# Convolution on VectorE, tokens scattered to regions per expert, and expert blocks started sequence by sequence

## The chip, the cores and the metric

The kernel runs on one core of one Trainium2 chip. The metric is the device time of the program in microseconds (us), median of the runs shown. One further execution was profiled; every duration below comes from it. Engines are named as in the profile: PE (TensorE; PEld its weight loads), DVE (VectorE), ACT (ScalarE), POOL (GpSimd) and SP (SyncE, which here only issues DMAs).

## What is computed

Eight sequences of 3584 tokens with 192 channels are convolved along time with 7 taps (a softmax of the weights, one set per head of 24 channels). Each convolved token is then sent to one of 8 experts, a two-layer network 192 to 1024 to 192 with ReLU, and scaled by its gate probability. A token takes the expert of its own best logit, unless its local gate is at least 0.5: then it takes the expert of the token before it.

```python
x_unf = x_pad[:, idx, :].reshape(B, S, K, H, group)          # causal window of 7
x = np.einsum('hk,bskhg->bshg', w, x_unf).reshape(B, S, D)
logits = np.einsum('bsd,de->bse', x, w_gate)
local_gate = 1.0 / (1.0 + np.exp(-np.einsum('bsd,de->bse', x, w_local).squeeze(-1)))
for b in range(B):
    prev_e = -1
    for s in range(S):
        fresh_e = int(np.argmax(logits[b, s]))
        e = fresh_e if s == 0 or local_gate[b, s] < 0.5 else prev_e
        prev_e = e
        h = np.maximum(x[b, s] @ w1[e], 0.0)
        out[b, s] = softmax(logits[b, s])[e] * (h @ w2[e])
```

## The kernel before

Three stages run one after the other; a scheduler sets the order of the instructions within each.

**Convolve and route** (`convolve_and_route`), over the sequences. `conv_bands` first builds banded 128 x 128 matrices on DVE and POOL (L73, L78, L80). A sequence lies in SBUF with tokens over partitions, 28 tiles of 128; PE multiplies it with the bands (L167, L169), ACT and DVE copy the result from PSUM into `y_sb` (L172, L174), PE transposes it (L180), ACT and DVE copy that (L184, L186), and PE forms the 9 logits (L189). `route` turns the logits into a one-hot of the expert per token with some 30 small DVE instructions and four tiny PE transposes; the carry of the expert from token to token is a running maximum over a key. The sequence goes to DRAM as `rows`.

**Place** (`place`), once, after all eight sequences: a running sum over all tokens gives each its slot, experts start at multiples of 256 slots, and 224 rounds of three DVE compares and one PE matmul (L355 to L361) turn "slot of token" into "token of slot", `slot_tok`. A block of 256 slots has one expert; there are 119 blocks.

**Experts** (`experts`), over the 119 blocks. Per block: SP loads the expert's weights `w1b` and `w2b` (L387, L389), POOL gathers 2 x 128 rows by `slot_tok` with indirect DMAs (L394); PE does the first layer (`hidden`: L415 on 128 channels, L424 on the other 64 in two 64-row tiles), the transposes of the next block (`turn`, L404), then the second layer (`output`, L439). ACT and DVE share the ReLU copies `hT` (L432, L430: two each) and the gated copies `o_sb` (L447, L445); DVE also copies the transposes, `xT` (L407). POOL scatters `o_sb` to the output with two indirect DMAs (L450). Weights are loaded two blocks ahead, with three buffers.

Of the kernel before, what the change touches and what calls it, by code (L numbers as in the profile page):

```python
# [9 lines left out]
BF16 = mybir.dt.bfloat16  # L10
# [39 lines left out]
def conv_bands(nc, cst, scr, weight):  # L50


    w = scr.tile([P, H, KC], F32, name="w")
    nc.sync.dma_start(out=w, in_=weight.partition_broadcast(P))
# [8 lines left out]
    c = scr.tile([P, H, KC], F32, name="c")  # L63
    nc.vector.tensor_tensor(c, w, bcast(ws, KC), op=Alu.mult)

    band = cst.tile([P, H, P], F32, name="band")
    pband = cst.tile([P, H, P], F32, name="pband")
    for dst, j0, shift in ((band, 0, 0), (pband, 1, P)):
        for j in range(j0, KC):

            m = scr.tile([P, P], F32, name="m", bufs=2)
            nc.gpsimd.memset(m, 0.0)
            nc.gpsimd.affine_select(out=m, in_=m, compare_op=Alu.not_equal, fill=1.0,  # L73
                                    base=shift - j, pattern=[[1, P]], channel_multiplier=-1)
            for h in range(H):
                tap = c[:, h, KC - 1 - j:KC - j]
                if j == j0:
                    nc.vector.tensor_scalar(dst[:, h, :], m, tap, None, Alu.mult)  # L78
                else:
                    nc.vector.scalar_tensor_tensor(dst[:, h, :], m, tap, dst[:, h, :],  # L80
                                                   Alu.mult, Alu.add)
    return band, pband
# [3 lines left out]
def kernel(  # L86
# [5 lines left out]
    w1: bass.AP,  # L92
    w2: bass.AP,
# [3 lines left out]
    keep = ctx.enter_context(tc.tile_pool(name="keep", bufs=1))  # L97
    dram = ctx.enter_context(tc.tile_pool(name="dram", bufs=1, space=DRAM))

    rows = dram.tile([N + 1, DG], F32, name="rows")  # L100

    ident = keep.tile([P, P], F32, name="ident")
    make_identity(nc, ident)

    oh_all = keep.tile([P, E, T], F32, name="oh_all")
    slot_tok = keep.tile([P, NS], I32, name="slot_tok")
    blk_e = keep.tile([1, NB], I32, name="blk_e")

    with ExitStack() as one:
        convolve_and_route(one, tc, x, weight, wgl, rows, ident, oh_all)  # L110
    with ExitStack() as two:
        place(two, tc, oh_all, slot_tok, blk_e)
    with ExitStack() as three:
        experts(three, tc, w1, w2, out, rows, ident, slot_tok, blk_e)


def convolve_and_route(ctx, tc, x, weight, wgl, rows, ident, oh_all):
    nc = tc.nc
    cst = ctx.enter_context(tc.tile_pool(name="cst", bufs=1))
    xs = ctx.enter_context(tc.tile_pool(name="xs", bufs=2))  # L120
    ys = ctx.enter_context(tc.tile_pool(name="ys", bufs=2))
    sm = ctx.enter_context(tc.tile_pool(name="sm", bufs=2))
    cps_p = ctx.enter_context(tc.tile_pool(name="cps_p", bufs=2, space=PSUM))
    tps_p = ctx.enter_context(tc.tile_pool(name="tps_p", bufs=2, space=PSUM))
    lps_p = ctx.enter_context(tc.tile_pool(name="lps_p", bufs=2, space=PSUM))
    rps_p = ctx.enter_context(tc.tile_pool(name="rps_p", bufs=1, space=PSUM))

    def load_x(b):
        x_sb = xs.tile([P, NT + 1, D], F32, name="x_sb")
        nc.gpsimd.memset(x_sb[:, 0, :], 0.0)  # L130
        for s in range(0, NT, CB):
            nc.sync.dma_start(out=x_sb[:, 1 + s:1 + s + CB, :],
                              in_=x[b, s * P:(s + CB) * P].rearrange("(j p) d -> p j d", p=P))
        return x_sb

    x_next = load_x(0)
    wg = cst.tile([DH, 2, E + 1], F32, name="wg")
    nc.scalar.dma_start(out=wg.rearrange("p k e -> p (k e)"), in_=wgl)
    zrow = cst.tile([1, DG], F32, name="zrow")
    nc.vector.memset(zrow, 0.0)  # L140
    nc.scalar.dma_start(out=rows[N:N + 1, :], in_=zrow)
    with tc.tile_pool(name="scr", bufs=1) as scr:
        band, pband = conv_bands(nc, cst, scr, weight)


    si = cst.tile([P, NT], I32, name="si")
    nc.gpsimd.iota(si, pattern=[[P, NT]], base=0, channel_multiplier=1)
    sf = cst.tile([P, NT], F32, name="sf")
    nc.vector.tensor_copy(sf, si)
    nc.vector.tensor_scalar(sf, sf, float(E), float(E + 1), Alu.mult, Alu.add)  # L150

    ii = cst.tile([P, E], I32, name="ii")
    nc.gpsimd.iota(ii, pattern=[[1, E]], base=0, channel_multiplier=0)
    ef = cst.tile([P, E], F32, name="ef")
    nc.vector.tensor_copy(ef, ii)
    ed = cst.tile([P, E], F32, name="ed")
    nc.vector.tensor_scalar(ed, ef, -1.0, float(E), Alu.mult, Alu.add)

    def conv(x_sb):
        y_sb = ys.tile([P, NT, DG], F32, name="y_sb")  # L160
        lps = lps_p.tile([P, NT, E + 1], F32, name="lps")
        for s in range(0, NT, CB):
            for h in range(H):
                hc = slice(h * GS, (h + 1) * GS)
                yc = slice(1 + h * GS, 1 + (h + 1) * GS)
                cps = cps_p.tile([P, CB, GS], F32, name="cps")
# [4 lines left out]
                if h % 2:  # L171
                    nc.vector.tensor_copy(y_sb[:, s:s + CB, yc], cps)  # L172
                else:
                    nc.scalar.copy(y_sb[:, s:s + CB, yc], cps)  # L174
            nc.gpsimd.tensor_copy(y_sb[:, s:s + CB, 1 + D:], y_sb[:, s:s + CB, 1 + P:1 + D])
        for j in range(0, NT, 2):
            tps = tps_p.tile([DH, 2, 2, P], F32, name="tps")
            for u in range(2):
                for k in range(2):
                    nc.tensor.transpose(tps[:, u, k, :], y_sb[:, j + u, 1 + k * DH:1 + (k + 1) * DH],  # L180
                                        identity=ident)
            yT = sm.tile([DH, 2, 2, P], F32, name="yT", bufs=3)
            if (j // 2) % 2:
                nc.vector.tensor_copy(yT, tps)  # L184
            else:
                nc.scalar.copy(yT, tps)  # L186
            for u in range(2):
                for k in range(2):
                    nc.tensor.matmul(lps[:, j + u, :], lhsT=yT[:, u, k, :], rhs=wg[:, k, :],  # L189
                                     start=(k == 0), stop=(k == 1))  # L190
        return y_sb, lps

    def route(b, y_sb, lps):
        lt = sm.tile([P, NT, E + 1], F32, name="lt")
# [25 lines left out]
        nc.vector.reciprocal(rs, rs)  # L220

        rps = rps_p.tile([P, 512], F32, name="rps")
        nc.tensor.transpose(rps[:NT, :P], key, identity=ident)
        row = sm.tile([NT, P], F32, name="row")
        nc.vector.tensor_copy(row, rps[:NT, :P])
        last = sm.tile([NT, 1], F32, name="last")
        nc.vector.tensor_reduce(last, row, axis=AX.X, op=Alu.max)
        nc.tensor.transpose(rps[:1, P:P + NT], last, identity=ident[:NT, :NT])  # L230
# [30 lines left out]
    for b in range(B):  # L261
# [4 lines left out]
        if held:  # L266
            route(b - 1, *held)
# [232 lines left out]
```

## Time and profile before

| | us |
|---|---|
| three runs, median (lowest to highest) | 1920.5 (1916.2 to 1920.5) |
| the profiled execution | 1925.5 |
| its span, first to last instruction | 1923.8 |
| PE busy | 1795.3 (93%) |
| DVE busy | 595.0 (31%) |
| ACT busy | 257.8 (13%) |
| POOL busy | 510.1 (27%) |
| bytes moved by DMA | 293.8 MB, 153 GB/s over the span |

The page cuts the span into 40 slices of 48 us. PE is at nine tenths or more in slices 13 to 39; before that its share swings, and its granted clock is at half of full speed in slices 9 to 12. DVE is at nine tenths in slices 10 and 11 alone. A span's busy share is a mean over three stages with different limits, so the reading below goes stage by stage. In a timeline row the columns are start, duration, engine, line, operation, out<-in, shapes, count, and in brackets the idle time before and what ended it.

### The profile page before, as it was taken

Reading aid. Unit: us, or ns where it says so; the run is one execution under the profiler, and the core shown is the slowest. Engines: PE = TensorE matmul, PEld = TensorE weight load, DVE = VectorE, ACT = ScalarE, POOL = GpSimd, SP = SyncE. Lnnn points to the kernel's source line nnn. Section 1 sums busy time; section 2 is a strip of 40 time slices with the busy share of each in tenths; the row PEclk is TensorE's granted clock in tenths of the full one; section 3 lists DMA queues with packets and bytes.
Section 4 is the critical chain, followed back from the end, with each engine's and each line's share of the span. In section 5 each row is a group of like instructions: output and inputs, shape, how many; then the busy total and the mean of one; then the engine's idle time right before and its main releaser. Section 6 shows DMA issues by size and latency. Waiting matters only on the chain. (4 is left out here: it accounts for less than half of the span.)

```text
span 1923.8 us, 26008 instructions
## 1 busy us (share of the span) xinstructions
PE 1795.3 (93%) x10208; PEld 1488.1 (77%) x10208; DVE 595.0 (31%) x1648; ACT 257.8 (13%) x487; POOL 510.1 (27%) x537
## 2 busy tenths in 40 slices
PE   2979797948979999999999999999999999999997
PEld 1768685841117988998898898898899889889887
DVE  6333333359982222222212212222222121221221
ACT  0212121200001111111111111111111111111111
POOL 3000000000003333333333333333333333333331
PEclk9979797955558999999999999999999999999999
DMA  3172736041006555556555555555555555555561
GB/s 115 58 205 72 202 101 169 1 124 30 1 27 220 187 177 186 187 173 188 178 181 187 177 186 183 180 188 173 189 185 175 186 178 184 185 179 186 178 184 42
DMA packets 115356, 293.76 MB, mean 153 GB/s; under 512 B 12639, under 2 KB 73559, under 8 KB 115234
## 3 DMA queue, kind: packets, MB, share of 16 engines
q1 hardware_dynamic: 63344, 209.24, 32.8%
q0 software_dynamic: 22848, 53.37, 9.3%
q10 hardware_dynamic: 29042, 29.48, 6.0%
q8 instruction: 81, 1.33, 0.3%
q14 instruction: 41, 0.34, 0.1%
HBM read 240.54 MB, written 52.87 MB: 153 GB/s over the span
## 5 line engine op out<-in xcount | busy, mean ns | idle before, releaser
L439 PE MATMUL yps<-w2b,hT 128*128 128x192 f32 x3808 | 638.8, 326 | 0.0
L439 PEld LDWEIGHTS yps<-w2b,hT 128*128 128x128 f32 x3808 | 616.0, 190 | 0.7 <-ACT hT L432 0.7
L450 POOL DMA_INDIRECT out_dram<-o_sb,slot_tok x238 | 240.7, 1011 | 796.5 <-ACT o_sb L447 678.4
L415 PE MATMUL hps<-xT,w1b 128*128 128x256 f32 x1904 | 432.6, 380 | 0.0
L415 PEld LDWEIGHTS hps<-xT,w1b 128*128 128x128 f32 x1904 | 360.2, 191 | 43.7
L430 DVE TENSOR_SCALAR hT<-hps 128x512 f32<-128x512 f32 x238 | 164.7, 692 | 460.9 <-PE hps L424 460.9
L394 POOL DMA_INDIRECT xg<-rows,slot_tok x238 | 233.3, 980 | 230.2 <-DVE slot_tok L369 154.4
L424 PE MATMUL hps<-xT,w1b 64*128 64x256 f32 x1904 | 237.7, 389 | 0.0
L432 ACT ACTIVATE hT<-hps 128x512 f32<-128x512 f32 x238 | 142.2, 598 | 696.0 <-PE hps L424 696.0
L445 DVE TENSOR_SCALAR o_sb<-yps,xg 128x192 f32<-128x192 f32 x119 | 49.7, 418 | 585.8 <-ACT o_sb L447 585.8
L424 PEld LDWEIGHTS hps<-xT,w1b 64*128 64x128 f32 x1904 | 174.1, 186 | 55.3 <-issue 39.5
L361 PE MATMUL sps<-at_hi,at_lo 128*128 128x476 bf16 x224 | 124.6, 556 | 25.6 <-DVE at_lo L355 14.2
L189 PEld LDWEIGHTS lps<-wg,yT 96*128 96x128 f32 x896 | 129.3, 218 | 16.6 <-ACT yT L186 8.0
L167 PE MATMUL cps<-x_sb,band 128*128 128x336 f32 x256 | 101.5, 481 | 40.0 <-DVE band L80 27.2
L447 ACT ACTIVATE o_sb<-yps,xg 128x192 f32<-128x192 f32 x119 | 50.1, 421 | 617.9 <-PE yps L439 607.5
L189 PE MATMUL lps<-wg,yT 96*128 96x9 f32 x896 | 125.6, 268 | 3.8 <-DVE yT L184 3.4
L361 PEld LDWEIGHTS <-at_lo 128*128 128x128 bf16 x224 | 23.3, 104 | 126.1 <-DVE at_lo L355 126.0
L169 PE MATMUL cps<-x_sb,pband 128*128 128x336 f32 x256 | 98.9, 470 | 10.2 <-DVE pband L80 10.2
L167 PEld LDWEIGHTS cps<-x_sb,band 128*128 128x128 f32 x256 | 48.8, 203 | 62.1 <-DVE band L80 27.4
L404 PEld LDWEIGHTS xps<-ident,xg 128*128 128x128 f32 x476 | 50.6, 142 | 51.4 <-DMA xg<-rows,slot_tok 38.0
L359 DVE TENSOR_SCALAR at_hi<-countb,hi,pf 128x238 bf16<-128x238 bf16 x224 | 90.1, 402 | 0.0
L404 PE MATMUL xps<-ident,xg 128*128 128x128 f32 x476 | 79.6, 289 | 10.7 <-DMA xg<-rows,slot_tok 10.7
(117 smaller groups left out, 713.3 us busy)
## 6 DMA issues: line engine op xcount, KB each, us to landing
w1b<-in_w_dram SPq DMA_DIRECT2D x119, 768.0 KB, 4.5
w2b<-in_w_dram SPq DMA_DIRECT2D x119, 768.0 KB, 4.5
rows<-y_sb ACTq DMA_DIRECT2D x16, 1799.0 KB, 11.3
x_sb<-in_x_dram SPq DMA_DIRECT2D x16, 1344.0 KB, 6.6
xg<-rows,slot_tok POOLq DMA_INDIRECT x238, 3.1
out_dram<-o_sb,slot_tok POOLq DMA_INDIRECT x238, 4.2
w<-in_weight_dram SPq DMA_DIRECT2D x1, 28.0 KB, 9.8
wg<-in_wgl_dram ACTq DMA_DIRECT2D x1, 6.8 KB, 3.9
```

The costliest lines, as they stand in the source:

```text
L167: nc.tensor.matmul(cps, lhsT=band[:, h, :], rhs=x_sb[:, 1 + s:1 + s + CB, hc], start=True, stop=False)
L169: nc.tensor.matmul(cps, lhsT=pband[:, h, :], rhs=x_sb[:, s:s + CB, hc], start=False, stop=True)
L189: nc.tensor.matmul(lps[:, j + u, :], lhsT=yT[:, u, k, :], rhs=wg[:, k, :], start=(k == 0), stop=(k == 1))
L361: nc.tensor.matmul(sps, lhsT=at_lo, rhs=at_hi, start=(t == 0), stop=(t == T - 1))
L394: nc.gpsimd.indirect_dma_start(out=xg[:, k, :], out_offset=None, in_=rows[:, :], in_offset=bass.IndirectOffsetOnAxis(ap=slot_tok[:, n:n + ...
L404: nc.tensor.transpose(xps[:, d, k * P:(k + 1) * P], xg[:, k, 1 + d * P:1 + (d + 1) * P], identity=ident)
L415: nc.tensor.matmul(hps[s // 2][:, s % 2, :], lhsT=w1b[:, s * P:(s + 1) * P], rhs=xT[:, 0, :], start=(s % 2 == 0), stop=False, skip_group_c ...
L424: nc.tensor.matmul(hps[half * 2 + row][:, j, :], lhsT=w1b[rows_, c:c + P], rhs=xT[rows_, 1, :], start=False, stop=True, skip_group_check=True)
L430: nc.vector.tensor_scalar(hT[:, 2 * q:2 * q + 2, :], hps[q], 0.0, None, Alu.max)
L432: nc.scalar.activation(hT[:, 2 * q:2 * q + 2, :], hps[q], Act.Relu)
L439: nc.tensor.matmul(yps[:, k, :], lhsT=hT[:, m, k * P:(k + 1) * P], rhs=w2b[:, m, :], start=(m == 0), stop=(m == FK - 1))
L450: nc.gpsimd.indirect_dma_start(out=out, out_offset=bass.IndirectOffsetOnAxis(ap=slot_tok[:, n:n + 1], axis=0), in_=o_sb[:, k, :], in_offse ...
```

## The change

The three stages become one program whose order is written out by hand (`tc.manual_schedule()`).

*Convolution.* Token s of a sequence now lies on partition s // 28, so that a window of 7 tokens lies in one partition (34 rows of x per partition, 6 of them a halo that repeats its neighbour's). Per head, ACT writes the first tap and DVE adds six (L192, L194); both write `y_sb` in place. The bands and the PE convolution are gone.

*Route.* PE transposes 42 tiles per sequence (L218), ACT copies them (L220), and the logits are formed with 32 columns of weights into four groups of 32 output partitions (L227). The carry of the expert uses two scans instead of the key. A running count `base` per expert gives each token of this sequence its slot at once, and POOL scatters the 28 tiles of `y_sb` into `slots`, a region per expert, with indirect DMAs (`put`, L333). Each row carries its gate and its token number. The `place` stage is gone; `blocks` (20 DVE instructions of 8 elements or fewer) lists the regions' full blocks after each sequence in a table `tabi`.

*Experts.* `load` reads the region and the expert of block i from the table, then issues one plain DMA for 256 rows and one for both weight matrices, all from SP. `FULL` is the number of blocks that must be full after each sequence whatever the routing: 7, 21, 35, 49, 63, 77, 91, and all 119 after the last. Two half-block steps are issued per block, one between `turn` and `output` and one behind `output`; a step is the next piece of the route of a sequence and, with it, three DVE taps of the convolution of the next one. If block i + 2 needs a sequence not yet routed, steps are issued until it is. Buffers of `xT`, `hT`, the PSUM tiles of `turn` and `output` go from 2 to 1, of `xg` from 4 to 3, of `o_sb` from 3 to 2. Every indirect DMA has a one-element POOL memset in front of it (`between`).

```diff
+def taps(nc, cst, scr, weight):
...
-                nc.tensor.matmul(cps, lhsT=band[:, h, :], rhs=x_sb[:, 1 + s:1 + s + CB, hc],
-                                 start=True, stop=False)
-                nc.tensor.matmul(cps, lhsT=pband[:, h, :], rhs=x_sb[:, s:s + CB, hc],
-                                 start=False, stop=True)
+                nc.scalar.activation(y, x_sb[:, t0:t0 + n, hc], Act.Copy, scale=c[:, h, 0:1])
+                for k in range(1, KC):
+                    nc.vector.scalar_tensor_tensor(y, x_sb[:, t0 + k:t0 + k + n, hc],
+                                                   c[:, h, k:k + 1], y, Alu.mult, Alu.add)
+                    yield
...
+        for t in range(NT):
+            between()
+            put = nc.gpsimd.indirect_dma_start(
+                out=slots[:, :], in_=y_sb[:, t, :], in_offset=None,
+                out_offset=bass.IndirectOffsetOnAxis(ap=posi[:, t:t + 1], axis=0))
+            placed(b, put)
+            if t == 0:
+                blocks(b)
+            if t % burst == burst - 1:
+                conv_ops()
+                yield
...
     def load(i):
+        ti = tabi[group_of[i]]
...
+        get = nc.sync.dma_start(
+            out=xg.rearrange("p k d -> p (k d)"),
...
+        nc.sync.dma_start(out=wb, in_=w12[bass.ds(e, 1)].rearrange("o p x -> (o p) x"))
...
+    PACE, BURST = 3, 3
+    state = {"conv": -1, "gen": None, "x": x_next, "route": -1, "rgen": None, "routed": -1}
...
+    start_conv()
+    while state["gen"]:
+        conv_ops()
+    while state["routed"] < 0:
+        step(2, 4)
+    while state["gen"]:
+        conv_ops()
+    for _ in range(9):
+        step(0, 4)
...
+    def ensure(i):
+        if i < NB and i not in ready:
+            while state["routed"] < group_of[i]:
+                step()
+            ready[i] = load(i)
...
     for i in range(NB):
+        ensure(i + AHEAD)
+        wb, xg = ready.pop(i)
+        hT = hidden(wb, xT)
         if i + 1 < NB:
+            xT = turn(ready[i + 1][1])
+        step()
+        output(wb, xg, hT)
+        step()
```

On DVE, around any expert block of the kernel before (L430 is the ReLU, L407 the copy `xT`, L445 the gated copy `o_sb`):

```order
L430 TENSOR_SCALAR hT_11428<-hps_11430 128x512
L430 TENSOR_SCALAR hT_11428<-hps_11432 128x512
L407 COPY xT_11458<-xps_11453 128x512
L445 TENSOR_SCALAR o_sb_11477<-yps_11460,xg_11289 128x192
L430 TENSOR_SCALAR hT_11496<-hps_11498 128x512
```

On DVE in the kernel after, just ahead of the ReLUs of block 25 (counted from 0): the end of the last routing step of sequence 3 and three taps (L194) of sequence 4.

```order
L378 TENSOR_TENSOR full<-full,eb 128x8
L380 SCALAR_TENSOR_TENSOR add<-full,pf,inn 128x8
L381 TENSOR_TENSOR add<-ef,inn 128x8
L382 COPY add<-inn 128x8
L384 TENSOR_REDUCE sums<-add 128x3
L385 TENSOR_TENSOR tab<-tab,sums 128x3
L386 COPY full<-nb 128x8
L387 COPY made<-end 128x1
L395 CAST tabi_3251<-tab 128x2
L194 SCALAR_TENSOR_TENSOR y_sb<-x_sb,c,y_sb 128x28x24 x3
L474 TENSOR_SCALAR hT<-hps 128x512 x2
L451 COPY xT<-xps 128x512
```

Between the `o_sb` of block 24 and these ReLUs (now L474) stand 6 taps and 31 routing instructions, where nothing stood before.

On PE, a block of the kernel before:

```order
L415 MATMUL hps<-xT,w1b 128x256 x8
L424 MATMUL hps<-xT,w1b 128x256 x8
L404 MATMUL xps<-ident,xg 128x128 x4
L439 MATMUL yps<-w2b,hT 128x192 x16
L415 MATMUL hps<-xT,w1b 128x256 x8
```

On PE in the kernel after, blocks 20 to 22 (L459 and L468 are the first layer, L448 `turn`, L483 the second layer):

```order
L448 MATMUL xps<-ident,xg 128x128 x4
L218 MATMUL bg<-ident,y_sb 128x128 x8
L483 MATMUL yps<-wb,hT 128x192 x16
L218 MATMUL bg<-ident,y_sb 128x128 x8
L459 MATMUL hps<-xT,wb 128x256 x8
L468 MATMUL hps<-xT,wb 128x256 x8
L448 MATMUL xps<-ident,xg 128x128 x4
L218 MATMUL bg<-ident,yr 128x128 x8
L483 MATMUL yps<-wb,hT 128x192 x16
L227 MATMUL bg<-yT,wg 32x256 x12
L459 MATMUL hps<-xT,wb 128x256 x8
```

The transposes and logits of a sequence have moved from the first stage into the gaps before and behind `output`.

On POOL, two blocks of the kernel before (L394 gathers, L450 scatters to the output):

```order
L394 DMA xg_11765<-rows_60,slot_tok_67 128x257 x2
L450 DMA out_0_dram<-o_sb_11681,slot_tok_67 28672x192
L450 DMA out_0_dram<-o_sb_11749,slot_tok_67 28672x192
L394 DMA xg_11833<-rows_60,slot_tok_67 128x257 x2
L450 DMA out_0_dram<-o_sb_11749,slot_tok_67 28672x192
```

On POOL in the kernel after, at block 19: the last of the 28 puts of sequence 2, which stand here in one run since block 21 needs that sequence, then the scatter of block 19.

```order
L108 MEMSET apart_102 1x1
L333 DMA slots_101<-y_sb_1272,posi_2481 229632x258
L185 IOTA y_sb_2643 128x28
L108 MEMSET apart_102 1x1
L495 DMA out_0_dram<-o_sb_2667,xg_2251 28672x192
```

The gathers have left POOL; the puts have come in, ahead of scatters.

## Rows read from the trace of the kernel before

**Rows 1.** Windows of the three stages; columns as the first line says
```profile
core 0: us, PE busy (x) PEld busy (x) DVE busy (x) ACT busy (x) POOL busy (x), PEclk, DMA share, GB/s
0.00:413.00 413.00, 336.14 (x1888) 270.04 (x1888) 152.87 (x459) 65.55 (x130) 32.21 (x58) 0.87 0.41 116
413.00:583.00 170.00, 128.09 (x237) 25.77 (x237) 157.18 (x714) 0.00 (x0) 11.74 (x11) 0.50 0.15 45
583.00:1914.00 1331.00, 1331.00 (x8086) 1192.33 (x8084) 284.51 (x474) 191.86 (x356) 464.22 (x466) 1.00 0.55 179
```

**Rows 2.** Timeline of PE: first and last expert block
```profile
583.07 5.89 PE L415 MATMUL hps<-xT,w1b 128*128 128x256 f32 x16
...
1908.58 5.47 PE L439 MATMUL yps<-w2b,hT 128*128 128x192 f32 x32
```

**Rows 3.** Timeline of PE and its weight loads in one block
```profile
1001.82 2.00 PE L424 MATMUL hps<-xT,w1b 64*128 64x256 f32 x16
1004.24 5.37 PE L439 MATMUL yps<-w2b,hT 128*128 128x192 f32 x32
...
1001.82 1.60 PEld L424 LDWEIGHTS hps<-xT,w1b 64*128 64x128 f32 x16 [0.33 <-issue]
1003.75 0.42 PEld L404 LDWEIGHTS xps<-ident,xg 128*128 128x128 f32 x4 [0.33 <-DMA xg<-rows,slot_tok]
...
1009.28 2.73 PEld L415 LDWEIGHTS hps<-xT,w1b 128*128 128x128 f32 x13
```

**Rows 4.** Timeline of DVE in the same block
```profile
1003.89 0.69 DVE L430 TENSOR_SCALAR hT<-hps 128x512 f32<-128x512 f32 x1 [0.17 <-PE hps L424]
1004.50 0.68 DVE L407 COPY xT<-xps 128x512 f32<-128x512 f32 x1
1010.10 0.42 DVE L445 TENSOR_SCALAR o_sb<-yps,xg 128x192 f32<-128x192 f32 x1 [4.92 <-ACT o_sb L447]
```

**Rows 5.** Groups by line: busy us, mean ns of one, idle before
```profile
L186 ACT COPY yT<-tps 96x512 f32<-96x512 f32 x56 | 32.6, 582 | 131.2 <-PE tps L180 131.2
L172 DVE COPY y_sb<-cps 128x336 f32<-128x336 f32 x64 | 32.5, 507 | 105.1 <-PE cps L169 103.1 <-DMA rows<-y_sb 2.0
L80 DVE SCALAR_TENSOR_TENSOR band<-m,c,band 128x128 f32<-128x128 f32 x48 | 13.0, 344 | 0.6 <-POOL m L73 0.6
L201 DVE TENSOR_TENSOR eq<-lt,mx 128x224 f32<-128x224 f32 x8 | 3.1, 392 | 0.0
L327 DVE TENSOR_TENSOR cum<-cum,base 128x1792 f32<-128x1792 f32 x1 | 2.0, 2026 | 0.0
L318 DVE CAST nb<-ni 128x8 f32<-128x8 int32 x1 | 0.2, 171 | 0.0
```

**Rows 6.** Timeline of DVE in `route`: each needs the one before
```profile
408.63 0.19 DVE L210 TENSOR_TENSOR key<-sf,key 128x28 f32<-128x28 f32 x1
408.85 0.19 DVE L211 TENSOR_TENSOR key<-key,fr 128x28 f32<-128x28 f32 x1
```

**Rows 7.** Timeline of DVE at the start: the softmax of the taps ends
```profile
13.60 0.22 DVE L64 TENSOR_TENSOR c<-w,ws 128x56 f32<-128x56 f32 x1
```

**Rows 8.** Timeline of POOL: indirect DMAs issued back to back
```profile
575.03 0.94 POOL L394 DMA_INDIRECT xg<-rows,slot_tok  x1 [0.30 <-issue]
576.28 0.95 POOL L394 DMA_INDIRECT xg<-rows,slot_tok  x1 [0.30 <-issue]
```

**Rows 9.** Timeline of the first 23 us: POOL selects alone and beside DVE
```profile
1.26 0.28 POOL masks.py:199 TENSOR_SCALAR_AFFINE_SELECT ident<-ident 128x128 f32<-128x128 f32 x1
...
17.80 4.32 DVE L80 SCALAR_TENSOR_TENSOR band<-m,c,band 128x128 f32<-128x128 f32 x16 [0.19 <-POOL m L73]
...
20.35 1.92 POOL L73 TENSOR_SCALAR_AFFINE_SELECT m<-m 128x128 f32<-128x128 f32 x1
```

**Rows 10.** DMA issues of the page: KB each, median us to landing
```profile
w1b<-in_w_dram SPq DMA_DIRECT2D x119, 768.0 KB, 4.5
...
xg<-rows,slot_tok POOLq DMA_INDIRECT x238, 3.1
out_dram<-o_sb,slot_tok POOLq DMA_INDIRECT x238, 4.2
```

More of the change, by code (lines that the diff above doesn't have):

```diff
@@ L62, in conv_bands @@
     nc.vector.reciprocal(ws, ws)
-    c = scr.tile([P, H, KC], F32, name="c")
+    c = cst.tile([P, H, KC], F32, name="c")
     nc.vector.tensor_tensor(c, w, bcast(ws, KC), op=Alu.mult)
[L66 to L82, printed above, removed]
+    return c
 @with_exitstack
@@ L109 @@
[L109 to L119, printed above, removed]
     xs = ctx.enter_context(tc.tile_pool(name="xs", bufs=2))
     ys = ctx.enter_context(tc.tile_pool(name="ys", bufs=2))
+    yt = ctx.enter_context(tc.tile_pool(name="yt", bufs=1))
@@ new lines, with between, load_x @@
+    hps_p = ctx.enter_context(tc.tile_pool(name="hps_p", bufs=4, space=PSUM))
+    yps_p = ctx.enter_context(tc.tile_pool(name="yps_p", bufs=1, space=PSUM))
+    ctx.enter_context(tc.manual_schedule())
+    slots = dram.tile([(DUMMY + 1) * BT, DG], F32, name="slots")
+    apart = cst.tile([1, 1], F32, name="apart")
+    def between():
+        nc.gpsimd.memset(apart, 0.0)
+    def load_x(b, cuts=(NX,)):
+        x_sb = xs.tile([P, NX, D], F32, name="x_sb")
+        src = x[b]
+        r0 = 0
+        for n, r1 in enumerate(cuts):
+            win = bass.AP(tensor=src.tensor, offset=src.offset + r0 * D,
+                          ap=[[NT * D, P], [1, (r1 - r0) * D]])
+            eng = nc.scalar if n % 2 else nc.sync
+            eng.dma_start(out=x_sb[:, r0:r1, :].rearrange("p t d -> p (t d)"), in_=win)
+            r0 = r1
+        return x_sb
@@ L138, in convolve_and_route @@
+    x_next = load_x(0, (NP + HALO, NX))
+    with tc.tile_pool(name="scr", bufs=1) as scr:
+        c = taps(nc, cst, scr, weight)
+    wg = cst.tile([P, 3, 32], F32, name="wg")
     nc.scalar.dma_start(out=wg.rearrange("p k e -> p (k e)"), in_=wgl)
[L139 to L150, printed above, removed]
+    ident = cst.tile([P, P], F32, name="ident")
+    make_identity(nc, ident)
+    ones = cst.tile([P, P], F32, name="ones")
+    nc.gpsimd.memset(ones, 1.0)
+    tri = cst.tile([P, P], F32, name="tri")
+    nc.gpsimd.affine_select(out=tri, in_=ones, compare_op=Alu.is_gt, fill=0.0,
+                            base=0, pattern=[[1, P]], channel_multiplier=-1)
@@ L220, in route @@
         nc.vector.reciprocal(rs, rs)
[L224 to L230, printed above, removed]
-        ends = sm.tile([1, NT], F32, name="ends")
@@ L401, in turn @@
+    def turn(xg):
         xps = xps_p.tile([P, 2, BT], F32, name="xps")
@@ new lines, in conv_ops, with step @@
+    def conv_ops(n=PACE):
+        for _ in range(n):
+            if state["gen"] is None:
+                return
+            if next(state["gen"], 0) == 0:
+                state["gen"] = None
+    def step(n=PACE, burst=BURST):
+        r = state["rgen"]
+        if r is None:
+            done = state["conv"] - (state["gen"] is not None)
+            if state["route"] + 1 <= done:
+                state["route"] += 1
+                r = state["rgen"] = route(state["route"], lambda: conv_ops(n), burst)
+        if state["gen"] is None and state["conv"] <= state["routed"] + 1:
+            start_conv()
+        if r is None:
+            conv_ops(n)
+        elif next(r, 0) == 0:
+            state["routed"] = state["route"]
+            state["rgen"] = None
```

525 lines of the change are left out of this document (293 added, 232 removed).

## The prediction

> **What bounds the kernel now.** I read the busy shares by stage first, since the page's 93% for PE is a mean over three different limits. [rows 1] shows them: 413 us in which PE is busy for 336, 170 us in which DVE is busy for 157 and PE runs at half clock, then 1331 us in which PE never rests, at full clock. Next I took PE's timeline at both ends of the last stage: first layer of block 0 at 583.07, last product ending at 1908.58 + 5.47 = 1914.05 [rows 2], so 119 blocks at 11.18 us. Then one block on each engine. PE runs through 64-row products, transposes and second layer without a gap [rows 3]. DVE works 0.69 + 0.69 + 0.68 + 0.42 = 2.5 of 11.2 us [rows 4]. So the expert blocks are bound by PE, and DVE has over 8 us free in each. The 583 us ahead of them are what can go, and the change can win at most what it hides there.
>
> **What goes.** All of the first 583 us is replaced by a shorter lead. The blocks keep their products, so 1331 us stay, and so does the tail, 1923.8 - 1914.0 = 10 us. The gathers leave POOL; since block data arrived in time before, that wins nothing by itself.
>
> **Price of a tap.** No row shows a two-input DVE instruction of 672 elements. The nearest is L80, 344 ns at 128 elements; the slope is (2026 - 392)/(1792 - 224) = 1.04 ns an element [rows 5]. That gives 0.56 us at 336 elements and 0.91 at 672. Each tap needs the one before it, and such neighbours start 0.22 us apart at 0.19 of work [rows 6], so 0.03 more: 0.59 and 0.94.
>
> **Price of a put.** Indirect DMAs leave POOL 1.25 us apart [rows 8]. Now a memset stands between, and DVE's taps run beside them. Lower bound 1.25. Upper bound 2.2, if each is held by one tap. I take 1.55, nearer the low end, because taps fill about half of DVE's time in the blocks and leave a gap after each.
>
> **The lead, step by step.** Taps' softmax ready as before, at 14 us [rows 7]; 11 small constants behind it at 0.17 [rows 5]: 16. Convolution of sequence 0, in halves: 96 taps at 0.59 = 57, so 73. Transposes and logits of its route: 42 transposes at about 0.21 (0.42/4 at full clock [rows 3], doubled, since PE comes from idle and block 0's first layer too took 5.89 us where 16 weight loads take 16 x 0.21 = 3.4 [rows 2, 3]), 14 ACT copies of 0.58 [rows 5], the logits, partly overlapped: 24, so 97. Behind that 36 small DVE instructions at about 0.3 and 6 taps: 16, so 113. Then 28 puts at 1.55: 43, so 157. Block 0 needs them landed (4.2 us [rows 10]), and its weights are issued behind its rows on SP, 1.5 MB where halves land in 4.5: 7 more. First layer at **168 us** instead of 583. Bounds: 159 with puts at 1.25, 186 at 2.2.
>
> **What PE gets in the blocks.** Sequences 2 to 7 are prepared there (1 for the most part in the lead). Each adds 42 transposes at 0.105 = 4.5 us; 48 instructions of logits; 4 + 7 small ones, 1.8; four changes of tile shape at 0.33 [rows 3], 1.3. The logits alone at 0.21 per 256 columns [rows 3] are 9.1. But 64-row products overlap in pairs: 16 in 2.00 us is 0.125 each [rows 3], 1.7 times as fast; I take that for the 32-column groups too: 5.3. Sum 12.9, six times: **77 us** (59 if four overlap fully, 100 if none).
>
> The Trainium skill (TensorEngine Tiling (Array Packing), section Tiling Modes) states that different tiles can load weights and multiply in parallel. By it the logits would take 2.3, an estimate that lowers the sum by 18 us; the trace shows pairs only, at 1.7 and not 2.
>
> **What stalls PE in the blocks.** Count from the end of `output` of the block before. PE passes the first layer (5.4), `turn` (0.5), a step (0.9), and needs DVE's first ReLU at 7.9. DVE ends `o_sb` at 0.9 [rows 3, 4], does 3 taps (2.8) and that ReLU (0.7): 4.4. So an ordinary pair of steps is hidden, with 3.5 us to spare. The exceptions:
> - The step that ends a routing holds 31 DVE instructions at about 0.22 and 6 taps, 12.5 us: ReLU at 14 instead of 7.9. Six us where it stands behind `output`, 4.6 ahead of it; sequences 3 to 6: 21.
> - PE's small transposes wait for the step before: 1.5 each, five times: 7.
> - Sequence 1 issues 4 puts a step. From 22 us after block 0 begins, POOL has 28 puts and 8 scatters, 36 x 1.55 = 56, so block 4's scatter ends at 78, not 59. Block 7 needs its `xg` buffer (three now). That DMA had 7.5 us to spare (scatter done 3 us after `output`, 4.2 to land, 3.1 for the rows [rows 10], `turn` at 17.8). 19 - 7.5: 11.
> - Sequence 2 is not ready when block 21 asks, so ten steps come at once at block 19. First put at 12, 28 puts 43, landing 4: 60. ACT's first tap of sequence 4 writes the buffer these puts read, and ACT's and DVE's ReLUs of block 20 queue behind it: 0.7, three taps, `o_sb`, three taps, ReLU, rest of `output`, 12 together. 72 us for what takes 24: 48.
> - Sequences 5 to 7 start in the same way behind the puts of 3 to 5: 9.5 + 36 x 1.55 + 4.2 = 69.5 where ACT arrives at 62.5, and its ReLU follows: 3.3 each, 10.
>
> Together **97 us** (about 60 at 1.25 a put, 160 at 1.9). SP's order hides: x is 3.3 MB once per sequence, ahead of a block's loads on SP, but weights are asked for two blocks ahead, and the DMA share was 0.55 [rows 1].
>
> **The sum.** 168 + 1331 + 77 + 97 + 10 = 1683 span. The profiled execution lies 1.7 above its span (1925.5 against 1923.8): 1685. The median of the runs lies 5.0 below that execution: **1680 us**, 0.875 of 1920.5.
>
> **Rivals.**
> - *POOL becomes the bound.* A POOL select of 0.28 us alone took 1.92 us while DVE ran 16 two-input instructions, and ended only after them [rows 9]. If indirect DMAs are held likewise, one tap each, a put costs 2.2. The lead then grows by 28 times the excess, sequences 1 and 2 by 36 and 28, sequences 3 to 6 by 36 each: 236 us per us, so 0.65 x 236 = 153: 1833. For it: those rows. Against: those 16 were independent and ran 0.27 apart without a gap, while taps wait for each other; and no row has an indirect DMA beside them. The Trainium skill (GPSIMD Engine Reference, section Key points) names this: POOL shares its SBUF interfaces with VectorE, and instructions with two SBUF inputs contend. The trace agrees for the select, 1.92 against 0.28.
> - *Faster.* Puts at 1.25 (-38) and logits fully overlapped (-18): 1624. For it: the spacing in [rows 8] holds at every pair there.
> - *Slower than before: taps over strided runs.* A tap reads and writes runs of 24 elements. Were it to cost 2.5 us, the lead grows by 126, the long steps by 38, sequence 2 by 19, and in some 44 blocks with taps in both steps the ReLU comes 2.9 late, 128: 1990. It decides from about 2.3 us a tap, 2.5 times my price. Against: L172 wrote 336 elements in the same runs of 24 in 507 ns [rows 5], the plain slope.
>
> **How the numbers follow.** Forecast 0.56, faster rival 0.22, POOL 0.15, slow taps 0.04; 0.03 for what I did not see. The range reaches from both low bounds and shorter waits, 1605, to puts at 1.9 (0.35 x 236 = 83) with the logits not overlapped (23), 1785; that leaves out most of the POOL case and the slow taps. About 0.3% is what a measurement of this kernel can tell from no change. Faster by more 0.95, within it 0.01, slower by more 0.04.
>
> **What would show it.** In the profile of the changed kernel: the first `hidden` near 168 us; taps at 0.91 us; POOL's indirect DMAs 1.4 to 1.7 us apart in the lead; ordinary blocks of the last 45 at 11.2 us; one hole of some 45 us on PE before block 21, with `xg` and ACT waiting for puts; about 6 us on DVE's ReLU once per sequence. The prediction is wrong if POOL is busy without a break through the first 70 blocks, if blocks without a routing step exceed 12.5 us, or if the hole at block 21 is missing.

## The result and the profile after

The changed kernel takes **1700.95 us**, median of four runs (1699.27 to 1704.2), against 1918.98 for the kernel before: a ratio of 0.887 (95% interval 0.885 to 0.889). That is 21 us above the forecast of 1680 and inside the range. The profiled execution has a span of 1698.9 us. Its page, first by engine, then in 40 slices:

```profile
PE 1460.1 (86%) x8900; PEld 1283.2 (76%) x8900; DVE 757.2 (45%) x1377; ACT 300.6 (18%) x559; POOL 562.6 (33%) x993
...
PE   0123899998498999899899899996999999999998
...
PEclk9966999999698999999899999997999999999999
```

Block 0 begins in the fifth slice, not after 583 us [rows 2]. What is left to see are the dips: one at slice 11, smaller ones later, most with a lower clock (PEclk) at the same place. The same by stage (length; busy us of PE, PEld, DVE, ACT and POOL with their instructions; granted clock; DMA share; GB/s):

```profile
0.00:172.00 172.00, 30.39 (x200) 19.74 (x200) 119.02 (x230) 30.05 (x58) 46.57 (x76) 0.81 0.30 115
172.00:253.50 81.50, 74.87 (x415) 64.26 (x416) 25.88 (x68) 9.80 (x18) 40.12 (x77) 0.93 0.54 188
253.50:331.70 78.20, 78.20 (x478) 70.10 (x477) 54.80 (x70) 16.55 (x28) 21.78 (x30) 1.00 0.57 205
395.90:477.00 81.10, 47.26 (x261) 41.06 (x259) 49.45 (x102) 12.74 (x23) 40.08 (x70) 0.75 0.38 140
...
1177.00:1690.70 513.70, 513.67 (x3126) 460.11 (x3124) 109.73 (x183) 74.36 (x138) 96.53 (x184) 1.00 0.49 175
```

The third row is blocks 6 to 12 with taps beside them: 78.2 busy of 78.2 us, so taps cost PE nothing there. The last row is blocks 73 to 118 with nothing beside them: 11.17 us each, as before [rows 2]. The fourth row is the hole of blocks 18 to 20, in which DVE, ACT and POOL are all partly idle.

The costs that the prediction had to bound, by line and form (instructions, then busy us, mean ns, idle time ahead of them and what ended it):

```profile
L194 DVE SCALAR_TENSOR_TENSOR y_sb<-x_sb,c,y_sb 128x672 f32<-128x672 f32 x336 | 319.4, 952 | 71.0 <-ACT y_sb L192 62.3
L194 DVE SCALAR_TENSOR_TENSOR y_sb<-x_sb,c,y_sb 128x336 f32<-128x336 f32 x96 | 55.8, 595 | 2.8
L333 POOL DMA_INDIRECT slots<-y_sb,posi x224 | 231.9, 1035 | 115.2 <-issue 65.1 <-DVE ni L364 49.9 <-DMA slots<-y_sb,posi 0.2
```

**Where the time went.** The start of each block's first layer, read from PE's timeline, gives each block's length; what it has over 11.17 us is its loss. Summed over stretches of blocks, for the first profile and for the same program run again later (e9, below):

| | predicted | first profile | e9 |
|---|---|---|---|
| first layer of block 0 at | 168 | 172.0 | 171.8 |
| 119 blocks | 1331 | 1329.2 | 1329.2 |
| transposes, logits, small waits of sequences 2 to 7 | 84 | 61.2 | 60.5 |
| hole at blocks 18 to 20 (without 4.0 of preparation) | 48 | 43.7 | 41.4 |
| long steps (blocks 25, 36, 46, 57, 67) | 21 | 39.1 | 36.5 |
| blocks 0 to 6 | 11 | 14.5 | 3.3 |
| first taps behind puts (blocks 26 to 28, 47 to 49) | 10 | 9.3 | 0 |
| blocks 68 to 79, behind the puts of padding | 0 | 21.7 | 9.6 |
| after the last product | 10 | 8.3 | 8.3 |
| sum (span) | 1683 | 1698.9 | 1660.5 |

Two rows of the first profile, blocks 0 to 6 and the first taps behind puts, are right only by their numbers: e9 is the same program and has little or nothing there. Three readings tell the cases apart.

The **hole**, in PE's and ACT's timeline (start, us, what, idle time ahead and what ended it):

```profile
414.49 0.57 PE L309 MATMUL bg<-mine,tri 128*128 128x8 f32 x2 [5.79 <-DVE mine L305]
...
435.30 1.97 PE L218 MATMUL bg<-ident,y_sb 128*128 128x128 f32 x8 [12.17 <-DVE y_sb L194]
...
463.81 1.11 PE L448 MATMUL xps<-ident,xg 128*128 128x128 f32 x4 [14.16 <-DMA xg<-slots]
```

```profile
461.22 0.86 ACT L192 ACTIVATE y_sb<-x_sb,c 128x672 f32<-128x672 f32 x1 [23.33 <-DMA slots<-y_sb,posi]
```

Ten steps come at once: PE first waits for the taps among them, then for rows that are still being put, and ACT's ReLU of block 20 stands behind a tap that waits for those puts, 23.3 us.

A **long step** on DVE and PE (block 25):

```profile
531.64 0.16 DVE L313 COPY num<-bg 128x16 f32<-128x16 f32 x1
...
538.63 2.81 DVE L194 SCALAR_TENSOR_TENSOR y_sb<-x_sb,c,y_sb 128x672 f32<-128x672 f32 x3
541.36 1.28 DVE L474 TENSOR_SCALAR hT<-hps 128x512 f32<-128x512 f32 x2
```

```profile
534.54 0.82 PE L483 MATMUL yps<-wb,hT 128*128 128x192 f32 x4
542.10 7.83 PE L483 MATMUL yps<-wb,hT 128*128 128x192 f32 x28 [6.74 <-DVE hT L474]
549.77 2.54 PE L459 MATMUL hps<-xT,wb 128*128 128x256 f32 x11
```

From 531.64 on DVE runs 31 small instructions and three more taps before the ReLU. PE waits 6.7 us (6 were predicted), and then 28 products take 7.8 us. The same 28 take 4.8 in e9's block 30, at full clock:

```profile
587.96 4.82 PE L483 MATMUL yps<-wb,hT 128*128 128x192 f32 x28 [0.34 <-DVE hT L474]
```

The windows of the changed kernel (columns as in the table by stage above) show the clock. It fell while PE still waited, and stayed at half for 10.2 us, 6.1 of them busy:

```profile
538.00:548.20 10.20, 6.10 (x19) 6.10 (x20) 7.77 (x16) 0.00 (x0) 4.79 (x10) 0.50 0.32 125
548.20:552.00 3.80, 3.80 (x22) 3.54 (x21) 1.25 (x2) 1.17 (x2) 1.09 (x3) 0.99 0.00 0
```

The block loses 10.1.

**Held instructions**, in block 72, on PE and ACT:

```profile
1158.29 0.58 PE L468 MATMUL hps<-xT,wb 64*128 64x256 f32 x1 [0.83 <-issue]
1160.38 0.58 PE L468 MATMUL hps<-xT,wb 64*128 64x256 f32 x1 [1.51 <-issue]
1162.48 0.58 PE L468 MATMUL hps<-xT,wb 64*128 64x256 f32 x1 [1.52 <-issue]
```

```profile
1168.15 0.42 ACT L492 ACTIVATE o_sb<-yps,xg 128x192 f32<-128x192 f32 x1 [27.98 <-remote]
```

These products wait for no semaphore in the program, yet start 1.4 to 2.1 us apart instead of 0.12 (16 in 2.00 us, [rows 3]). ACT's `o_sb` waits for products that PE ended at 1145.3. In the trace's records SP's register moves, 0.03 us at the median, take 0.70 in 7 of 240 cases, and with SP's other short instructions there are 28 such, in 13 places, all beside puts. No row of the kernel before has that.

### The profile page after: what moved, and what is told of

Same layout as the page of the kernel before. It is cut to its first block, busy times and chain, and to the rows that moved or that the text cites. A ratio compares the mean times of both kernels' runs of the same rounds, so it can differ in the third digit from the quotient of the medians.

```text
span 1698.9 us, 23730 instructions
## 1 busy us (share of the span) xinstructions
PE 1460.1 (86%) x8900; PEld 1283.2 (76%) x8900; DVE 757.2 (45%) x1377; ACT 300.6 (18%) x559; POOL 562.6 (33%) x993
## 3 DMA queue, kind: packets, MB, share of 16 engines
q10 hardware_dynamic: 576, 1.72, 0.3%
## 4 chain that ended last, share of the span: by engine, by line
issue 28%; PE 25%; POOL 11%; DVE 6%; DMA 1%; ACT 1%; POOLq 0%; another core or an unknown queue 0%; ACTq 0%; DVEq 0%
PE yps L483 12%; PE hps L459 7%; POOL out_dram L495 6%; PE hps L468 4%; POOL slots L333 3%; DVE y_sb L194 3%; PE bg L218 1%; PE xps L448 1%; POOL slots L415 1%; PE bg L227 1%; POOL apart L108 1%; DMA slots<-y_sb,posi 1%; DVE hT L474 0%; POOLq L495 0%; ACT y_sb L192 0%
## 5 line engine op out<-in xcount | busy, mean ns | idle before, releaser
L483 PE MATMUL yps<-wb,hT 128*128 128x192 f32 x3808 | 663.5, 333 | 32.5 <-DVE hT L474 22.3
L483 PEld LDWEIGHTS yps<-wb,hT 128*128 128x128 f32 x3808 | 635.8, 195 | 40.0 <-DVE hT L474 25.2
L495 POOL DMA_INDIRECT out_dram<-o_sb,xg x238 | 246.1, 1034 | 903.4 <-ACT o_sb L492 865.5
L459 PE MATMUL hps<-xT,wb 128*128 128x256 f32 x1904 | 440.2, 384 | 11.0 <-issue 6.1
L194 DVE SCALAR_TENSOR_TENSOR y_sb<-x_sb,c,y_sb 128x672 f32<-128x672 f32 (+1 forms) x432 | 375.3, 873 | 73.8 <-ACT y_sb L192 62.3
L459 PEld LDWEIGHTS hps<-xT,wb 128*128 128x128 f32 x1904 | 360.3, 192 | 61.7 <-issue 14.4
L474 DVE TENSOR_SCALAR hT<-hps 128x512 f32<-128x512 f32 x238 | 162.6, 690 | 307.6 <-PE hps L468 265.7
L333 POOL DMA_INDIRECT slots<-y_sb,posi x224 | 231.9, 1035 | 115.2 <-issue 65.1
L468 PE MATMUL hps<-xT,wb 64*128 64x256 f32 x1904 | 244.3, 391 | 11.6 <-issue 11.5
L468 PEld LDWEIGHTS hps<-xT,wb 64*128 64x128 f32 x1904 | 177.1, 187 | 70.3 <-issue 54.6
L218 PE MATMUL bg<-ident,y_sb 128*128 128x128 f32 x224 | 35.8, 307 | 128.4 <-DVE y_sb L194 122.7
L218 PEld LDWEIGHTS bg<-ident,y_sb 128*128 128x128 f32 x224 | 29.3, 158 | 131.8 <-DVE y_sb L194 71.7
L448 PEld LDWEIGHTS xps<-ident,xg 128*128 128x128 f32 x476 | 50.7, 142 | 55.5 <-issue 38.1
L448 PE MATMUL xps<-ident,xg 128*128 128x128 f32 x476 | 79.1, 289 | 15.6 <-DMA xg<-slots 15.6
L451 DVE COPY xT<-xps 128x512 f32<-128x512 f32 x119 | 81.2, 682 | 18.5 <-remote 15.7
L220 ACT COPY yT<-bg 128x512 f32<-128x512 f32 x96 | 47.3, 535 | 117.9 <-PE bg L218 115.7
L192 ACT ACTIVATE y_sb<-x_sb,c 128x672 f32<-128x672 f32 (+1 forms) x72 | 55.0, 792 | 32.4 <-DMA slots<-y_sb,posi 26.1
```

The costliest lines, as they stand in the source:

```text
L194: nc.vector.scalar_tensor_tensor(y, x_sb[:, t0 + k:t0 + k + n, hc], c[:, h, k:k + 1], y, Alu.mult, Alu.add)
L218: nc.tensor.transpose(tps[:, j, q * P:(q + 1) * P], src, identity=ident)
L333: put = nc.gpsimd.indirect_dma_start(out=slots[:, :], in_=y_sb[:, t, :], in_offset=None, out_offset=bass.IndirectOffsetOnAxis(ap=posi[:, t ...
L448: nc.tensor.transpose(xps[:, d, k * P:(k + 1) * P], xg[:, k, Y0 + d * P:Y0 + (d + 1) * P], identity=ident)
L451: nc.vector.tensor_copy(xT, xps)
L459: nc.tensor.matmul(hps[s // 2][:, s % 2, :], lhsT=wb[:, s * P:(s + 1) * P], rhs=xT[:, 0, :], start=(s % 2 == 0), stop=False, skip_group_ch ...
```

## Experiments

Twelve runs, in three groups: e1 to e4 on one chip, e5 to e8 on a second, e9 to e12 on a third. The chip of the first result is not on record. e4 and e5 were run once, the others four times. "Loses" means over 11.17 us, as above. Each of e1 to e4 has 6 to 9 of SP's register moves at 0.70 us, as the first profile has, and none of e5 to e12 has one. So e1 to e4 are set against the first profile, the later runs against e9. The kernel before takes the same beside all three groups, 1924.5, 1923.7 and 1924.4 us.

**e1: taps from block 0 on.** In the changed kernel the steps of sequence 1's routing that are left for the blocks keep the number of taps of the lead, none.

```diff
+        state["n"] = n
...
-                r = state["rgen"] = route(state["route"], lambda: conv_ops(n), burst)
+                r = state["rgen"] = route(state["route"], lambda: conv_ops(state["n"]), burst)
```

> The steps left over from sequence 1's routing take three taps each again, so sequence 2 is convolved about 27 taps (4.5 blocks) earlier. Theory (the hole before block 21 is there only because sequence 2 is late): the 47.8 us that blocks 18 to 20 lose to 11.17 us each fall to about 5 of preparation, nothing else moves: 1658 us. Rival (the taps beside sequence 1's puts hold POOL, and the wait moves to blocks 2 to 6): 30 of the 43 come back there: 1690 us.

1669.6 us (ratio 0.867, interval 0.866 to 0.869). Blocks 18 to 20 lose 5.5 instead of 47.7, and blocks 0 to 6 lose 15.4 instead of 14.5: the hole was there only because sequence 2 was late. Of the 42 us, 31 show: sequence 2's own long step, which stood inside the hole, now loses 8.1 in block 15.

**e2: the long step cut.** A `yield` behind `posi`; `blocks(b)` with a step of its own behind the puts.

```diff
         nc.vector.tensor_copy(posi, pos)
+        yield
...
-            if t == 0:
-                blocks(b)
...
+        blocks(b)
+        yield
```

> The step that ends a routing is cut: nine small VectorE instructions, then five and the first puts, and the nineteen that make the table of blocks in a step of their own behind the puts. Theory (blocks 25, 36, 46, 57 and 67 lose 39 us because VectorE's ReLU is queued behind 31 small instructions and 6 taps, and because TensorE then falls to half clock): about 30 us less, 1671 us, and no ReLU wait over 1.5 us there. Rival (the loss is made by the puts that POOL issues in a row, not by the queue on VectorE): 10 us at most, 1691 us.

1681.8 us (0.873, 0.871 to 0.876). What PE waited for DVE's ReLU, in the waits (us in total, times, longest), of the changed kernel and of e2:

```profile
PE yps L483 <- DVE hT L474: 22.3, 9, 6.7
```

```profile
PE yps L484 <- ACT hT L477: 24.2, 4, 11.2
...
PE yps L484 <- DVE hT L475: 3.8, 4, 1.7
```

The wait for DVE is gone, as the theory says; blocks 25 and 36 lose 0.1 and 0.6. But six other blocks (5, 30, 53, 62, 72, 78) lose 56 us together: in each ACT waits 4 to 17 us, "remote", past the end of PE's products, as in block 72 of the changed kernel. So the cause of the long step's loss is settled. Of the 30 us that were expected 19 show; that held instructions took the rest is read from these waits and not tested.

**e3: padding two a step.** `fill` yields after every second put.

> The 16 puts of padding that come in one step after sequence 7 are spread, two a step. Theory (44 indirect DMAs in a row on POOL bring about the 20.7 us that block 72 loses): 18 us less, 1683 us, with at most 1 us lost in each of the next four blocks. Rival (each of these puts costs the other engines its share, wherever it stands): the loss is only spread over blocks 72 to 76, 1701 us.

1681.4 us (0.873, 0.872 to 0.875). Blocks 68 to 79 lose 2.0 instead of 21.7. It was the row of 44, not each put. This run does not tell whether the row acts through held instructions or through POOL's order.

**e4 and e5: bursts of extra puts** in blocks where nothing is prepared, with what the blocks behind each lost:

> Extra puts of padding rows into a region of their own, in blocks where nothing is prepared: 4, 8 and 16 in a row behind blocks 80, 83 and 87 (rows in range), the same behind 92, 95 and 99 with every index out of range, two a step (16 in all) in blocks 104 to 107, and 16 in a row without the memsets between behind block 110. Theory A (a long row of indirect DMAs on POOL slows the instructions of all other engines): 4 cost nothing, 8 one to three us, 16 ten to twenty, and the spread ones nothing: some 40 to 60 us more than 1701. Rival B (only the order on POOL matters, buffers come free late): 16 x 1.28 us are up before a buffer is missed, so none of them costs anything: 1701 us. Rival C (only indices out of range do it): the bursts of 92, 95 and 99 cost what A says, those in range nothing: 1720 us.

> Extra puts again, all with every index out of range, in blocks where nothing is prepared: 16 in a row of 128 rows behind block 80, 16 of 64 rows behind 87, 32 of 64 rows behind 94, 16 of 128 rows with a memset of 512 elements ahead of each behind 102, 28 of 128 rows behind 110. Theory A1 (what counts is the number of indirect DMA instructions in a row): 16 cost 13 us with 64 rows as with 128, 32 of 64 rows over 25. Theory A2 (what counts is the number of rows): 16 of 64 rows cost 2 us, as 8 of 128 did, and 32 of them 13. Both: with the memset between, under 5 us, and 28 in a row 20 to 25.

| burst | e4 | e5 |
|---|---|---|
| 4 in a row, in range / out of range | 0 / 0 | |
| 8, in range / out of range | 2.2 / 1.9 | |
| 16, in range / out of range | 10.2 / 13.4 | / 4.4 |
| 16, no memset between | 14.2 | |
| 16 over four blocks, two a step | 0.9 | |
| 16 of 64 rows / 32 of 64 rows | | 5.1 / 23.4 |
| 16, longer memset between (1.72 us apart) | | 12.6 |
| 28 | | 23.2 |

In e4 the losses are those of theory A, in range or not, with the small memset or not (1749.5 us, 49 over the first result), so rival C is out. In e5 (1729.7 us) a second mechanism is at work. PE behind 16 puts in e4, and behind 16 and then 32 in e5:

```profile
1380.09 0.38 PE L459 MATMUL hps<-xT,wb 128*128 128x256 f32 x1 [1.10 <-issue]
1382.17 0.38 PE L459 MATMUL hps<-xT,wb 128*128 128x256 f32 x1 [1.71 <-issue]
```

```profile
1257.85 0.63 PE L448 MATMUL xps<-ident,xg 128*128 128x128 f32 x4 [2.66 <-DMA xg<-slots]
...
1441.95 1.08 PE L448 MATMUL xps<-ident,xg 128*128 128x128 f32 x4 [20.91 <-DMA xg<-slots]
```

In e5 PE waits for rows: the scatters stand behind the burst on POOL, they hold a rows buffer, and the next load comes late. The number of instructions counts (A1), since an indirect DMA takes nearly as long for 64 rows as for 128 (1.21 us from start to start for 1.28), but 16 cost 4 to 5 us and not 13, and the memset between made it worse, not better: what counts is how long POOL is taken. That is rival B of e4, with 16 puts already too many; it had said none would cost anything. And e5's first 80 blocks, the same program, lose 152 where the first profile loses 190.

**e9, e10, e11: the changed kernel again, beside two edits of one number.** e6 is the first run of the same edit as e10.

> The changed kernel itself, not edited, on the same chip as the next three. In its first profile SP's register moves, which take 0.03 us, took 0.70 us in 13 places beside POOL's puts, and every other engine was late there; in the run with the second set of bursts, whose first 80 blocks are the same program, blocks 0 to 6, 26 to 28 and 47 to 49 lost 2.7 us together instead of 23.9, and block 73 lost 11 where block 72 had lost 21. Theory (that slowness belongs to the chip or the session, not to the program): either 1700 us with it or about 1662 us without it, by what this chip shows. Rival (it belongs to the program): 1700 us in any case.

> Two puts a step instead of three, nothing else. Theory (what blocks 27, 36, 48 and 57 lose over VectorE's long step, and most of block 72, comes from puts that POOL issues without a gap): with four puts and two scatters in 11.2 us POOL has 3.5 us of pause in each block; about 9 us less at 27 and 48 and 7 less at 72, where 16 puts of padding are left in a row: 1683 us. Rival (each put costs its share wherever it stands, or the wait is ACT's first tap behind the last put): 1701 us, with the loss only moved.

> Two puts a step once more, now beside the unedited kernel on one chip. Theory (where instructions are not held at 0.70 us the puts' rhythm matters only through POOL's order, which delays the scatters and so the next rows): 2 to 8 us less than the run before it if that run shows no such instructions, about 20 less if it does. Rival (fewer puts in a row are worth the 41 us between 1701 and 1660): 41 us less.

> Four buffers of rows (xg) instead of three, nothing else. Theory (44 indirect DMAs in a row keep block 71's scatters back, these keep its rows' buffer, and TensorE waits 8 us for the rows of a later block and then runs at half clock): that block's 11 us go, as does what is left of the same wait elsewhere; the hole before block 21 stays: 10 to 13 us less than the unedited kernel beside it. Rival (the loss there is instructions held by POOL's puts): no change.

e9 takes **1663.5 us** (0.865, 0.863 to 0.867), the theory's 1662: the same program is 37 us quicker here, and SP has no register move of 0.70 us. Of the records of PE's semaphore updates the first profile lacks 50 of 866, e1 to e4 39 to 72, e5 to e12 none; so where instructions are held, records are lost too. Block 73 of e9, with nothing held:

```profile
1132.54 2.00 PE L468 MATMUL hps<-xT,wb 64*128 64x256 f32 x16
1142.61 1.09 PE L448 MATMUL xps<-ident,xg 128*128 128x128 f32 x4 [8.08 <-DMA xg<-slots]
```

Two puts a step: 1659.9 (e6) and 1659.2 us (e10), 4 less than e9, as the theory has it. Compared with the first result, e6 alone would have passed for a gain of 41 us.

Four `xg` buffers (e11): 1661.4 us, 2 less, where 10 to 13 were expected; the runs of e9 and e11 overlap. Block 73 loses nothing any more, so that cause was right; but block 30 loses 7.8 instead of 2.4, and block 41 4.9 instead of 2.4. In block 30 ACT's first tap of a sequence waits 6.6 us for puts instead of 2.8, and PE for ACT's and DVE's ReLU. The blocks did not come earlier (block 29 begins at 568.2, in e9 at 567.9). What came earlier is SP's load of the next x, 3.3 MB. SP's x, POOL's last put and ACT's tap, in e9 and in e11:

```profile
573.72 0.43 SPq L119 DMA_DIRECT2D x_sb<-in_x_dram  x1
575.18 0.96 POOL L333 DMA_INDIRECT slots<-y_sb,posi  x1 [0.22 <-issue]
583.59 0.86 ACT L192 ACTIVATE y_sb<-x_sb,c 128x672 f32<-128x672 f32 x1 [2.79 <-DMA slots<-y_sb,posi]
```

```profile
568.79 0.42 SPq L119 DMA_DIRECT2D x_sb<-in_x_dram  x1
575.49 0.96 POOL L333 DMA_INDIRECT slots<-y_sb,posi  x1 [0.22 <-issue]
587.68 0.86 ACT L192 ACTIVATE y_sb<-x_sb,c 128x672 f32<-128x672 f32 x1 [6.59 <-DMA slots<-y_sb,posi]
```

The last put leaves POOL at the same time, but the tap is let go 4.1 us later. The fourth buffer let SP run ahead, and the DMA share is 0.95 to 1.05 from 571 to 589. That the puts landed late behind x is the likely reading; no run tests it.

**e7, e8, e12: together.** e7 has e1, a cut long step with `blocks(b)` in the third step of puts, e3, two puts a step from sequence 3 on, and a sequence's first tap two steps later. e8 asks for the taps' weights ahead of x. e12 adds a fourth `xg` buffer and takes the taps out of the step of `lt`.

```diff
...
+    w_sb = cst.tile([P, H, KC], F32, name="w")
+    nc.scalar.dma_start(out=w_sb, in_=weight.partition_broadcast(P))
     x_next = load_x(0, (NP + HALO, NX))
...
```

> All edits together: taps go on from block 0, the long step is cut and the table of blocks made in the third step of puts (which has no taps), from sequence 3 on two puts a step, padding two a step, and a sequence's first tap two steps later. If the losses are separate, 172 to the first layer, 119 x 11.17 = 1329, 63 of preparation, 14 beside sequence 1's puts, some 10 of small waits and 10 at the end are left: 1600 us. Rival (the puts cost the other engines the same in whatever rhythm they come): 1640 us.

> As the one before, and the taps' weights are asked for ahead of x. Theory (the lead is late by the 9 us that VectorE waits for these weights, 21 us instead of 12): first layer 8 us earlier, 1592 us. Rival (the first tap then waits for x, which lands at about 20 us): within 1 us of the one before.

> All edits and the weights first, with four buffers of rows, and without taps in the step whose small VectorE instructions TensorE's next transposes wait for. Theory: block 6's wait for rows (9.0 us and half clock behind it) goes, 11 us; the waits of 2.9 us in blocks 37 and 64 and of 1.3 in four others go, 10 us: 1564 us. Rival (the weights' or the outputs' buffers are late next): 1574 us.

e7: **1596.0 us** (0.830, 0.828 to 0.831), 4 off the expected 1600: the losses are separate. One term of that sum came true by luck: the 14 us beside sequence 1's puts, for the most part held instructions in the first profile, are here mostly a wait of 9.8 us for block 7's rows. e8: 1584.4; DVE's first instruction, in the changed kernel and in e8:

```profile
21.10 0.21 DVE L61 TENSOR_REDUCE wm<-w 128x8 f32<-128x56 f32 x1 [21.10 <-DMA w<-in_weight_dram]
```

```profile
9.74 0.21 DVE L59 TENSOR_REDUCE wm<-w 128x8 f32<-128x56 f32 x1 [9.74 <-DMA w<-in_weight_dram]
```

11.4 us earlier, and 11.6 less in all. e12: **1579.4 us** (0.821, 0.819 to 0.822), the best, but 5 less than e8 instead of 20. The waits of PE's small transposes shrank in blocks 13, 23, 37, 50 and 64, 10 us as expected. But the taps that were taken out of that step run in later ones: blocks 24 and 51 lose 6 us more, where PE now waits for the next small steps, as in block 24:

```profile
468.15 0.19 PE L289 MATMUL bg<-ident,so_far 1*128 1x1 f32 x1 [1.19 <-DVE so_far L281]
```

The wait in block 6 did not shrink:

```profile
243.84 1.09 PE L452 MATMUL xps<-ident,xg 128*128 128x128 f32 x4 [9.58 <-DMA xg<-slots]
```

Block 7 is the first with rows of sequence 1, and the last of those puts leaves POOL only at 238.3. What was late there is the data, not a buffer.

## Why the prediction was right, and where it was not

- **The lead** came at 172.0 for 168. Taps cost 0.595 and 0.952 us for 0.59 and 0.94; the first 96 took 58.6 for 57. Its first term failed: the weights' softmax was taken "as before, at 14 us", but in the new program the weights come behind 3.3 MB of x, and taps start at 23.5 (e8 shows the price, 11.5 us). Transposes, logits and small steps took 37.6 us up to the first put (82.1 to 119.7) where 40 were summed, and from the end of the last put to the first layer it took 8.8 us for 11; that hid half of it. Puts were 1.58 apart in the lead for 1.55. That is right only as a mean: they were 1.27 apart wherever no taps ran, and mostly 1.8 to 1.9 beside taps.
- **The blocks** kept 11.17 us, as said.
- **What PE gets** was too dear: 61 with the small waits for 84. The logits are the largest term, some 14 of these 23 us: the 24 products of 256 columns of a sequence's first half, on four tiles of 32 columns, took 1.50 us, 0.06 each, where 0.125 was taken and 0.21 is the price of one alone [rows 3]. The Trainium skill (TensorEngine Tiling (Array Packing), section Tiling Modes) has them run in parallel; the trace agrees, at 3.4 of 4. The rival named faster had this half right; its other half, puts at 1.25, came true only without taps beside them.
- **The hole** was right in place, cause and size (44 for 48; e1). The prediction's single hole on PE is three, of 5.8, 12.2 and 14.2 us.
- **The long steps** were right in the wait and wrong in the price. PE waits 6.7 us in blocks 25 and 46 and 4.9 in 36 and 57 (there in two parts, for DVE's `o_sb` and then for its ReLU), for 6 and 4.6. The missing term is the clock: during each of these four waits the granted clock falls to the lower of its two levels for 3.4 to 10.2 us, and each block loses 1.9 to 3.4 us beyond its wait, 12 of the 18 us by which these steps were dearer than the forecast. Sequence 7's step (block 67), which has no taps and was not counted, lost 3.9. Over all blocks PE is busy 62.6 us at half clock, which is up to 31 us of the sum by an estimate that halves them; in e9 it is 36.1 us. The Trainium skill (TensorE: Matmul & The Clock Gate, section HAM oscillation) says that gaps throttle PE again; the trace agrees (0.50 from 538.0 on, above). The prediction had the row for it in block 0 [rows 2] and used it in the lead alone.
- **Sequence 1's puts** were predicted to make block 7's rows late by 11 us. In e9 they did not make them late: no taps ran beside them, so they stood 1.27 apart, not 1.55, and blocks 2 to 6 lose nothing. With taps beside them (e7, e8, e12) the wait is there, 9 to 10 us, for the rows themselves and not for a buffer. In e1, which has taps there too, blocks 2 and 3 are 10 us late themselves, and block 6 loses 1.0. Of the 14.5 of the first profile 11 are held instructions, since e9 loses 3.3.
- **First taps behind puts** cost nothing in e9; the 9.3 us of the first profile are held instructions again.
- **Padding** was overlooked: 16 puts in one step behind sequence 7's 28. It is 9.6 us in e9 through POOL's order, 21.7 in the first profile.
- **Rivals.** That taps make POOL the bound did not come, but its mechanism is there: a put beside taps takes up to 1.6 us instead of 0.97, and puts stand 1.9 apart, where 2.2 was feared. Only about half of the lead's puts have taps beside them, and fewer in the blocks. Strided taps at 2.5 us did not come. The 38 us that the faster rival takes for puts at 1.25 do not fit the prediction's own bounds, which give 9 in the lead and 37 in the stalls; nothing else hangs on it.

In the spans the first profile is 16 us above the sum: 22 of padding, 18 of long steps, 4 of lead and 3 of the first blocks more, 23 of preparation, 4 of the hole and 4 of smaller terms less. The other 5 are the step from a span to the median: it was taken as 3 less and is 2 more. That errors of this size nearly cancel is luck. Beside e9, without held instructions, the forecast is 16 us too high.

**Open.** What holds the instructions at 0.70 us. They come with rows of indirect DMAs on POOL, in the first profile and on the chip of e1 to e4, hardly on the two other chips, with records lost beside them. Whether the chip or the time of the run makes the difference no run tells. The Trainium skill (NOTIFIC — the notification-queue block, section Overflow: three behaviours, one of which stalls the engine) states that a full record queue can be set to stall its producer. Every run here was recorded, so none shows whether an execution without recording has it.

## What to carry to other kernels

An engine's free time is not enough to hide work on it: ask what is queued behind each hidden step, and add to every stall of TensorE what the clock takes with it. A queue that both feeds and drains a loop (here POOL, puts and scatters) wants its long jobs cut into pieces that fit between two drains, and a planner's burst should be timed against the block that needs its data. Before a gain of two per cent is believed, run the unedited kernel again beside it: here two sets of runs of the same program, each steady to 0.3%, lay 37 us apart.

## What was not expected of the hardware

- Indirect DMAs in a row left POOL 1.27 us apart with 128 rows, also with all indices out of range, and 1.21 with 64 rows. Beside taps it was up to 1.9.
- PE's granted clock fell to half during waits of 4.9 to 6.7 us and stayed there for 3.4 to 10.2 us.
- In the first profile and on the chip of e1 to e4, beside these DMAs, instructions of PE, ACT and SP were held, SP's moves at 0.70 us for 0.03 (in e4 four DMAs in a row cost nothing, eight about 2 us, sixteen 10 to 14). The identical program in e9 showed no such move and was 2.2% quicker, while the kernel before took the same to 0.3% beside both.
